# Second products of the first sub-block on whole float32 operands instead of float32r high and low parts

## The chip, the cores and the metric

The kernel runs on one core of a Trainium2 chip. The core has TensorE for matrix products (PE in the profile, its weight loads PEld), VectorE (DVE), ScalarE (ACT), GpSimd (POOL), and SyncE (SP), from whose queue the transfers start. The metric is device time in microseconds (us), from one execution of the whole program. Lower is better.

## What is computed

Chunked attention (64 tokens to a chunk, 8 heads of 64), and on its output a mixture of four experts, all in float32:

```python
scores = scale * np.matmul(q_c, k_c.transpose(0, 1, 2, 4, 3))
attn = softmax(scores)                       # with 1e-9 added to the sum
x = np.matmul(attn, v_c) ...                 # x: 4608 tokens x 512
p = domain_probs / (domain_probs.sum(-1, keepdims=True) + 1e-09)
for e in range(4):
    h = np.maximum(x @ w1[e], 0.0)           # w1[e]: 512 x 1024
    out += p[:, e:e + 1] * (h @ w2[e])       # w2[e]: 1024 x 512
```

## The kernel before

A float32 value is held as two float32r parts: the high part is what a copy into a float32r tile leaves (ACT, `hi_part`), the low part is the value less the high part (POOL or DVE, `lo_part`). A product of two such pairs is three products of parts, high by high, high by low and low by high, summed in one PSUM bank. `TERMS` at line 459 lists the three; `product` at line 463 issues one `nc.tensor.matmul` for each entry of its list, and every one of them shows up as line 465 in the profile.

The 4608 tokens are cut into 9 sub-blocks of 512. Weights are taken in 8 passes (4 experts, each in two halves of 512 hidden units; `n_pass` is 8, `n` counts passes on through the whole run). The first sub-block goes alone, in passes 0 to 7 (`startup` and `plain_pass`); the other eight go in four pairs, by a seven-product scheme on 2 by 2 blocks (`Group`, `Outer`). While PE works on the first sub-block, the attention of the first pair is computed beside it: its small steps are put between the large products by `Beside.go`, at a fixed rate. Nothing is reordered at run time; the program order on each engine is that in which the Python code issues the work.

A plain pass of the first sub-block has eight steps. Four steps are hidden blocks (`plain_hidden`, 128 hidden units by 512 tokens, twelve products each), whose result is put through ReLU by `relu_parts`: ACT writes the high part (line 472), DVE the low part (line 473). Four steps are token tiles (`Tile.whole`, 128 tokens by 512 outputs): for each of the four hidden blocks the transposed h is the stationary operand, 128 by 128, and a row block of w2 the moving one, 128 by 512. With three terms that is twelve products for a tile. Pass 0 issues tile 0 in three pieces instead, in `startup`, and the last tile of pass 7 is held back and issued as `held` within the first pass of the pairs. `Tile.out` then adds the tile, scaled by its probability, on DVE (lines 760 and 762). The pairs' own passes 8 to 15 use `Tile` as well, for 8 tiles each.

The parts of w2 are made from the loaded quarters (`raw`, tile `wraw`) by `w2_split`: four ACT copies (line 278) and four subtractions on POOL (line 281) a pass, 128 by 512 each. The tiles of h and of w2 share a family of names: `hfh0` to `hfh3` and `hfl0` to `hfl3` hold h, `hfh4`, `hfh5`, `hfl4` and `hfl5` hold w2, so that in the trace a product of a token tile reads `hfh,hfh`, `hfl,hfh` or `hfh,hfl` (names are shown without their numbers; the first is the stationary operand or the moving one, in no order that matters here). Products of hidden blocks read `xh,wf` or `xl,wf`.

Some products run on whole float32 operands already: the attention's scores (`a_scores` line 140, `start_scores` line 832) and values (`a_values` line 169, `start_values` line 852), 64 by 64 by 64 each, one call a product, and the transposes (lines 160 and 838, 128 by 128).

`product` and the two functions that set the size of the work to be followed:

```python
TERMS = ((0, 0), (0, 1), (1, 0))
...
def whole(self):
    self.part(range(NK), slice(0, dm), True, True)
```

Of the kernel before, what the change touches and what calls it, by code (L numbers as in the profile page):

```python
# [8 lines left out]
F32 = mybir.dt.float32  # L9
# [6 lines left out]
P = 128  # L16
C = 64
SUB = 512
# [12 lines left out]
def chunk_attention_moe(ctx: ExitStack, tc: tile.TileContext, qk, v, v0, dp, w1, w2, out):  # L31
# [14 lines left out]
    n_pass = 2 * n_exp  # L46
# [9 lines left out]
    hpool = ctx.enter_context(tc.tile_pool(name="hpool", bufs=1))  # L56
# [202 lines left out]
    raw = {}  # L259
    w1t, w2t = {}, {}  # L260
# [16 lines left out]
    def hi_part(src, t):  # L277
        nc.scalar.copy(out=t[0], in_=src)  # L278
# [21 lines left out]
    def w2_quad(f, k):  # L300
        return [t[:, :, f * 2 * P : (f + 1) * 2 * P] for t in w2t[k]]

    def w2_split(f, k, eng=None):
        if f == 0:
            w2t[k] = [hpool.tile([P, 2, SUB], F32R, name=f"hf{part}{4 + k}") for part in ("h", "l")]
        split(eng or nc.gpsimd, raw[1, f, k], w2_quad(f, k))

    class Factors:


# [157 lines left out]
                skip_group_check=not (first and last),  # L468
            )

    def relu_parts(src, hi, lo):
        nc.scalar.activation(out=hi, in_=src, func=AF.Relu)
        nc.vector.scalar_tensor_tensor(
            out=lo, in0=src, scalar=0.0, in1=hi.bitcast(F32), op0=ALU.max, op1=ALU.subtract
        )
# [2 lines left out]
    hs = {}  # L478
    acc = {}

    def h_alloc(s, f):
        i, k = divmod(f, 2)
        if k == 0:
            hs[s, i] = [hpool.tile([P, 2, SUB], F32R, name=f"hf{part}{2 * s + i}") for part in ("h", "l")]
        return h_part(s, f)

# [4 lines left out]
    def plain_hidden(f, tiles, alloc=True, order=BY_BLOCK, name=None):  # L491
        cols = slice(tiles[0] * P, (tiles[-1] + 1) * P)
        if alloc:
            h_alloc(0, f)
        out = bank(name)[:, : cols.stop - cols.start]
        product(
            out, order,
            lambda k, a: w1t[f // 2, k // 2][a][:, f % 2, k % 2],
            lambda k, b: xt["plain"][b][:, k, cols],
        )  # L500
        relu_parts(out, *(part[:, cols] for part in h_part(0, f)))
# [225 lines left out]
    class Tile:  # L727
# [7 lines left out]
        def part(self, fs, cols, first, last):  # L735
            if first:
                self.ps = bank(self.name)[:, : cols.stop - cols.start]
            product(
                self.ps, [(f, a, b) for f in fs for a, b in TERMS],
                lambda f, a: h_part(self.s, f)[a][:, self.i * P : (self.i + 1) * P],  # L740
                lambda f, b: w2t[f // 2][b][:, f % 2, cols],
                first=first, last=last,
            )
            if last:
                self.out(cols)
# [127 lines left out]
    def start_hidden(u, fs, lo):  # L873

        for a in range(1 if lo else 2):
            for f in fs:
                begin = u == 0 and not lo and a == 0
                if begin:
                    hidden[f] = bank(("C0", "C1", "A0", "B0")[f])[:, first]
                    h_alloc(0, f)  # L880
                product(
                    hidden[f], [(k, a, int(lo)) for k in (2 * u, 2 * u + 1)],
                    lambda k, a: w1t[f // 2, k // 2][a][:, f % 2, k % 2],
                    lambda k, b: xt["plain"][b][:, k, first],
                    first=begin, last=u == 1 and lo,
                )
# [36 lines left out]
    def startup(beside):  # L923
        load_all()
        x_alloc(0)

        nc.scalar.activation(out=small.tile([P, 1], F32, name="first"), in_=zeros[:, :1], func=AF.Exp)
        keep_warm(WAITS["loads"])
        start_scores(0)
        less_max(sc[0])  # L930
        a_exp(sc[0])
        start_scores(1)
        start_weights(0)
        less_max(sc[1])
        keep_warm(WAITS["softmax"])
        start_transpose(0)
        a_exp(sc[1])
        w1_split(0, 0, nc.gpsimd)
        keep_warm(WAITS["copy"])
        start_values(0)  # L940
        hi_part(*start_x(0))
        w1_split(1, 0, nc.gpsimd)
        start_weights(1)
        start_hidden(0, (0, 1), False)
        lo_part(nc.vector, *start_x(0))
        start_transpose(1)
        start_hidden(0, (0, 1), True)
        w1_split(0, 1, nc.gpsimd)
        start_scores(2)
        less_max(sc[2])  # L950
        start_values(1)
        hi_part(*start_x(1))
        a_exp(sc[2])
        start_hidden(0, (2, 3), False)
        start_hidden(0, (2, 3), True)
        w1_split(1, 1, nc.gpsimd)
        lo_part(nc.vector, *start_x(1))
        start_weights(2)
        w_load(1, 0, 0, 1)
        w_load(1, 0, 1, 1)  # L960
        start_v(2)
        w2_split(0, 0)
        w2_split(1, 0)
        start_hidden(1, (0, 1), False)
        start_hidden(1, (0, 1), True)
        for f in range(2):
            start_relu(f)
        w2_split(0, 1)
        w2_split(1, 1)
        start_scores(3)  # L970
        less_max(sc[3])
        start_hidden(1, (2, 3), False)
        start_transpose(2)
        start_hidden(1, (2, 3), True)
        for f in range(2, NK):
            start_relu(f)
        a_exp(sc[3])
        start_weights(3)
        norm_probs()
        o = tiles(0, 0, range(NT), ("C0", "C1", "C1", "A1"))  # L980
        o[0].part((0, 1), slice(0, dm), True, False)
        start_values(2)
        split(nc.vector, *start_x(2))
        o[0].part((2,), slice(0, dm), False, False)
        start_transpose(3)
        o[0].part((3,), slice(0, dm), False, True)
        start_values(3)
        split(nc.vector, *start_x(3))
        o[1].whole()
        beside.load()  # L990
        w_loads(0, 1)
        for f in range(NK):
            plain_hidden(f, [2, 3], alloc=False, name=("B1", "B0", "A0", "C0")[f])
        for i, (f, k) in enumerate(QUADS):
            w1_split(f, k, (nc.gpsimd, nc.vector)[i % 2])
        w_loads(1, 1)
        for i in range(2, NT):
            o[i].whole()
# [36 lines left out]
    def plain_pass(n, beside, x, ahead_of=None):  # L1035

        at = {}
        o = tiles(0, n, range(NT), ("A1", "B1", "C0", "C1") if ahead_of else None)
        steps = [lambda f=f: plain_hidden(f, range(NT)) for f in range(NK)]
        steps += [i.whole for i in o]  # L1040
        order = PAIR_QUADS if ahead_of else QUADS
        for i in range(NK):
            add(at, i // 2, lambda i=i: w2_split(*QUADS[i]))
            add(at, i // 2, lambda i=i: w_load(0, n + 1, *order[i]))
        if n == 2:
            add(at, 1, probs_by_expert)
            add(at, 5, transpose_probs)
        if not ahead_of:
            for i, (f, k) in enumerate(QUADS):
                add(at, (3, 4, 4, 5)[i], lambda f=f, k=k: w1_split(f, k, nc.gpsimd))  # L1050
            add(at, 5, lambda: w_loads(1, n + 1))
            if x:
                add(at, 0, x.sum1)
                add(at, 1, x.sum3, lambda: x.hi("t1"))
                add(at, 2, lambda: x.lo("t1"), lambda: x.hi("b22"))
                add(at, 4, lambda: x.lo("b22"))
                add(at, 5, x.sum2, lambda: x.hi("t3"))
                add(at, 6, lambda: x.lo("t3"), lambda: x.hi("t2"))
                add(at, 7, lambda: x.lo("t2"))
            issue(steps, at, beside, True)  # L1060
            return None, None
        w = []
        add(at, 0, x.sum4, lambda: x.hi("t4"))
        add(at, 1, lambda: x.lo("t4"))
        add(at, 2, lambda: w.append(Factors(0)), lambda: w[0].sum1(), lambda: w[0].sum2())
        add(at, 3, lambda: w[0].hi("a11"), lambda: w[0].hi("s2"), lambda: x.hi("b11"))
        add(at, 3, lambda: w[0].lo("a11"), lambda: w[0].lo("s2"), lambda: x.lo("b11"))
        add(at, 4, lambda: w[0].hi("a12"), lambda: x.hi("b21"), lambda: w[0].hi("s1"))
        add(at, 4, lambda: w[0].lo("a12"), lambda: x.lo("b21"), lambda: w[0].lo("s1"))
        add(at, 5, lambda: w[0].hi("a22"), lambda: w[0].lo("a22"))  # L1070
        add(at, 5, lambda: w[0].sum3(), lambda: w[0].sum4())
        add(at, 2, ahead_of.load)
        add(at, 6, lambda: w_loads(1, n + 1, order))
        issue(steps[:-1], at, beside, True)
        return steps[-1], w[0]
# [362 lines left out]
```

## Time and profile before

| | |
|---|---|
| median of two runs | 1515.2 us (1514.97 and 1515.43) |
| the profiled execution's own time | 1515.59 us |
| its span, first to last instruction | 1513.8 us |
| PE busy | 1505.7 us, 99% of the span, 8854 instructions |
| DVE, ACT, POOL busy | 918.6, 572.9 and 871.7 us |
| first sub-block | from the start to about 214 us |

The profile is that of one execution. A row of a group names the line of the kernel, the engine, the operation, the tiles as out<-in, shapes and types, the count, then the busy time, the mean duration of one in ns, and the idle time before. The durations of matmuls overlap on a pipelined PE: how long one occupies PE is read from the distance between starts, not from its duration. float32r operands of a product are printed as f32 in the PE rows, like float32 ones. In the timeline a row is a run of like instructions: start, length, engine, line and what it does.

### The profile page before, as it was taken

What the parts mean: (1) busy time and instruction counts of PE and PEld (TensorE: products, weight loads), DVE (VectorE), ACT (ScalarE), POOL (GpSimd) and SP (SyncE); (2) the same over time, 40 slices, a digit from 0 to 9 for tenths busy, and PEclk for the clock granted to TensorE, in tenths of its full rate; (3) what the DMA queues carried; (4) which work ended last, traced back from release to release, by engine and by line L of the source; (5) the groups of instructions that cost most, each with busy time, mean ns of one, the idle gap of its engine ahead of it and who ended that gap; (6) DMA issues with size and microseconds to landing.
All of it is one profiled execution on the core that took longest, in us unless ns stands there. A gap on an engine that the chain in (4) does not pass through costs nothing.

```text
span 1513.8 us, 23370 instructions
## 1 busy us (share of the span) xinstructions
PE 1505.7 (99%) x8854; PEld 1238.8 (82%) x8855; DVE 918.6 (61%) x1289; ACT 572.9 (38%) x1000; POOL 871.7 (58%) x666
## 2 busy tenths in 40 slices
PE   9999999999999999999999999999999999999998
PEld 7888888888888888888888888888888888888887
DVE  5443554444444465776766956666668756666665
ACT  3333444344444334333333444333333443333332
POOL 2443588677766616555556754555557555555554
PEclk9999999999999999999999999999999999999999
DMA  6443359877767576767665677676666676666664
GB/s 197 133 156 125 106 167 310 274 251 243 231 234 238 187 266 215 230 209 228 205 203 189 216 226 243 205 229 209 212 190 200 204 231 201 201 200 201 200 191 145
DMA packets 167936, 314.17 MB, mean 208 GB/s; under 512 B 14208, under 2 KB 84112, under 8 KB 167824
## 3 DMA queue, kind: packets, MB, share of 16 engines
q1 hardware_dynamic: 167824, 312.68, 63.7%
q8 instruction: 70, 1.15, 0.3%
q14 instruction: 42, 0.34, 0.1%
HBM read 244.39 MB, written 68.23 MB: 207 GB/s over the span
## 4 chain that ended last, share of the span: by engine, by line
PE 99%; DVE 0%; ACT 0%; issue 0%; ACTq 0%
PE A L465 49%; PE C L465 29%; PE B L465 16%; PE psa L169 1%; PE psa L140 1%; PE psa L160 1%; PE psa L780 0%; PE C L901 0%; PE B L852 0%; PE A L832 0%; PE C L780 0%; PE A L852 0%; PE psa L832 0%; PE B L838 0%; PE psa L838 0%; PE B L780 0%
## 5 line engine op out<-in xcount | busy, mean ns | idle before, releaser
L647 POOL TENSOR_TENSOR hfl<-wraw,hfh 128x512 fp32r<-128x512 f32 x288 | 374.4, 1316 | 216.2 <-ACT hfh L644 214.0
L465 PE MATMUL A<-xh,wf 128*128 128x512 f32 (+1 forms) x1104 | 379.5, 389 | 0.0
L465 PE MATMUL A<-hfh,wf 128*128 128x512 f32 (+1 forms) x768 | 270.6, 394 | 0.0
L644 ACT CAST hfh<-wraw 128x512 fp32r<-128x512 f32 x288 | 176.4, 622 | 208.5 <-DVE wraw L638 59.7
L465 PEld LDWEIGHTS A<-xh,wf 128*128 128x128 f32 x1104 | 206.8, 188 | 43.1
L527 ACT COPY s<-A 128x512 f32<-128x512 f32 x192 | 112.8, 587 | 329.7 <-PE A L465 328.9
L465 PE MATMUL A<-xl,wf 128*128 128x512 f32 (+1 forms) x552 | 213.7, 388 | 0.0
L465 PE MATMUL C<-xh,wf 128*128 128x512 f32 (+1 forms) x600 | 204.0, 388 | 0.7 <-ACT xh L278 0.7
L465 PEld LDWEIGHTS A<-hfh,wf 128*128 128x128 f32 x768 | 144.1, 188 | 31.0 <-DVE acc L694 1.2
L694 DVE TENSOR_TENSOR acc<-A,acc 128x512 f32<-128x512 f32 x174 | 119.2, 686 | 78.7 <-PE A L465 78.2
L465 PE MATMUL A<-hfl,wf 128*128 128x512 f32 x384 | 149.4, 389 | 0.0
L465 PE MATMUL C<-hfh,wf 128*128 128x512 f32 x384 | 133.9, 390 | 0.0
L281 POOL TENSOR_TENSOR hfl<-wraw,hfh 128x512 fp32r<-128x512 f32 x64 | 85.9, 1372 | 80.5 <-ACT hfh L278 80.5
L465 PEld LDWEIGHTS C<-xh,wf 128*128 128x128 f32 x600 | 111.5, 188 | 23.9 <-ACT xh L278 0.8
L465 PE MATMUL B<-xh,wf 128*128 128x512 f32 (+1 forms) x376 | 125.3, 384 | 0.0
L281 POOL TENSOR_TENSOR wf<-wraw,wf 128x512 fp32r<-128x512 f32 x70 | 91.5, 1330 | 53.4 <-ACT wf L278 53.2
L465 PEld LDWEIGHTS A<-xl,wf 128*128 128x128 f32 x552 | 103.5, 188 | 21.1
L465 PE MATMUL C<-xl,wf 128*128 128x512 f32 (+1 forms) x300 | 114.7, 385 | 0.0
L638 POOL TENSOR_TENSOR wf<-wraw,wf 128x512 f32<-128x512 f32 x23 | 29.7, 1291 | 145.2 <-DVE wf L632 145.2
L694 DVE TENSOR_TENSOR acc<-C,acc 128x512 f32<-128x512 f32 x90 | 62.2, 691 | 64.3 <-PE C L465 58.7
L647 POOL TENSOR_TENSOR hfl<-wf,hfh 128x512 fp32r<-128x512 f32 x48 | 71.2, 1483 | 38.9 <-ACT hfh L644 38.6
L465 PEld LDWEIGHTS C<-hfh,wf 128*128 128x128 f32 x384 | 72.1, 188 | 14.9
(186 smaller groups left out, 2727.7 us busy)
## 6 DMA issues: line engine op xcount, KB each, us to landing
wf<-w SPq DMA_DIRECT2D x336, 512.0 KB, 4.1
wraw<-in_w SPq DMA_DIRECT2D x128, 256.0 KB, 4.0
w<-wf SPq DMA_DIRECT2D x112, 256.0 KB, 4.7
qk_in<-in_qk SPq DMA_DIRECT2D x32, 512.0 KB, 5.4
v_in<-in_v SPq DMA_DIRECT2D x32, 256.0 KB, 4.4
w<-hfl SPq DMA_DIRECT2D x32, 256.0 KB, 2.7
w<-hfh SPq DMA_DIRECT2D x32, 256.0 KB, 2.9
w<-hfh SPq DMA_DIRECT2D x48, 128.0 KB, 2.7
```

The lines of the kernel that those rows point to most:

```text
L140: nc.tensor.matmul(s["sc"][half, c, j], lhsT=s["x"][rows, g, 0, h], rhs=s["x"][rows, g, 1, h], start=True, stop=True,)
L160: nc.tensor.transpose(ps[:, j], s["e"][:, j].rearrange("p c k -> p (c k)"), ident)
L169: nc.tensor.matmul(av[half, c, j], lhsT=s["v"][rows, 2 * j + odd], rhs=s["pt"][rows, j, half], start=True, stop=True,)
L281: eng.tensor_tensor(out=t[1], in0=src, in1=t[0].bitcast(F32), op=ALU.subtract)
L465: nc.tensor.matmul(out, lhsT=lhs(k, a), rhs=rhs(k, b), start=first and i == 0, stop=last and i == len(parts) - 1, skip_group_check=not (fi ...
L527: nc.scalar.copy(out=t, in_=self.a)
L638: (eng or nc.vector).tensor_tensor(out=self.values[place, k], in0=self.values[a, k], in1=self.values[b, k], op=op)
L644: nc.scalar.copy(out=self.part(name, 0)[:, k], in_=self.values[name, k])
L647: (eng or nc.gpsimd).tensor_tensor(out=self.part(name, 1)[:, k], in0=self.values[name, k], in1=self.part(name, 0)[:, k].bitcast(F32), op=A ...
L694: nc.vector.tensor_tensor(out=acc[key], in0=src, in1=acc[key], op=ALU.add)
```

## The change

In passes 0 to 7, h and w2 of the token tiles are kept as one float32 tile each in place of a float32r pair. `relu_parts` writes one part and returns; `w2_whole` takes the place of `w2_split` and copies the quarter on ACT, with no subtraction on POOL; `Tile.part` issues one product a hidden block on these float32 operands in place of three. The hidden blocks' own products stay as they are, and so does everything from pass 8 on.

```diff
+    def w2_whole(f, k):
+
+        if f == 0:
+            w2t[k] = [hpool.tile([P, 2, SUB], F32, name=f"hfh{4 + k}")]
+        hi_part(raw[1, f, k], w2_quad(f, k))
+
...
-    def relu_parts(src, hi, lo):
+    def relu_parts(src, hi, lo=None):
         nc.scalar.activation(out=hi, in_=src, func=AF.Relu)
+        if lo is None:
+            return
         nc.vector.scalar_tensor_tensor(
...
-    def h_alloc(s, f):
+    def h_alloc(s, f, whole=False):
         i, k = divmod(f, 2)
-        if k == 0:
+        if k == 0 and whole:
+            hs[s, i] = [hpool.tile([P, 2, SUB], F32, name=f"hfh{2 * s + i}")]
+        elif k == 0:
             hs[s, i] = [hpool.tile([P, 2, SUB], F32R, name=f"hf{part}{2 * s + i}") for part in ("h", "l")]
...
-            h_alloc(0, f)
+            h_alloc(0, f, True)
...
-                self.ps, [(f, a, b) for f in fs for a, b in TERMS],
+                self.ps, [(f, a, b) for f in fs for a, b in (TERMS if self.n >= n_pass else TERMS[:1])],
...
-        w2_split(0, 0)
-        w2_split(1, 0)
+        w2_whole(0, 0)
+        w2_whole(1, 0)
...
-            add(at, i // 2, lambda i=i: w2_split(*QUADS[i]))
+            add(at, i // 2, lambda i=i: w2_whole(*QUADS[i]))
```

The second `h_alloc(0, f, True)` is in `start_hidden`, and the other two `w2_split` calls of `startup` become `w2_whole` likewise.

More of the change, by code (lines that the diff above doesn't have):

```diff
@@ L879, in start_hidden @@
                     hidden[f] = bank(("C0", "C1", "A0", "B0")[f])[:, first]
-                    h_alloc(0, f)
+                    h_alloc(0, f, True)
                 product(
@@ L967, in startup @@
             start_relu(f)
-        w2_split(0, 1)
-        w2_split(1, 1)
+        w2_whole(0, 1)
+        w2_whole(1, 1)
         start_scores(3)
```

## The prediction

> **What bounds the kernel now.** I began with the page's first part and its chain of work, to see which engine sets the end.
>
> ```profile
> span 1513.8 us, 23370 instructions
> PE 1505.7 (99%) x8854; PEld 1238.8 (82%) x8855; DVE 918.6 (61%) x1289; ACT 572.9 (38%) x1000; POOL 871.7 (58%) x666
> PE 99%; DVE 0%; ACT 0%; issue 0%; ACTq 0%
> ```
>
> PE is busy in all but 8 us, and the chain that ended last lies on PE from end to end. The list of waits of PE says how much another engine could still give back.
>
> ```profile
> PE C L901 <- DVE s L895: 1.2, 1, 1.2
> PE A L832 <- DMA xraw<-in_qk: 0.9, 1, 0.9
> PE C L465 <- ACT xh L278: 0.7, 1, 0.7
> PE B L838 <- DVE e L198: 0.4, 1, 0.4
> PE B L1358 <- DVE acc L1352: 0.2, 1, 0.2
> PE C L901 <- issue: 0.2, 1, 0.2
> ```
>
> That is 3.6 us in all, and none of it is a wait for a low part of h or of w2. So the time of the change is the time that PE itself gains or loses on the token tiles. Last I looked at how the products of those tiles follow each other, in the chain in order of time and in the timeline around the end of the stage.
>
> ```profile
> 178.34 5.44 PE C L465 x24
> 183.78 5.44 PE A L465 x24
> ...
> 211.07 0.39 PE L465 MATMUL C<-hfh,hfh 128*128 128x512 f32 x1
> 211.07 0.19 PEld L465 LDWEIGHTS C<-hfl,hfh 128*128 128x128 f32 x1
> ```
>
> The two pieces of the chain are token tiles, two to a piece, with 24 products in 5.44 us: one float32r product of 512 columns occupies PE for 226.7 ns, and a tile of twelve for 2.72 us. The last two rows show that the weights of the next product are loaded while the present one streams.
>
> **What is removed from PE.** The instructions that touch a low part of h or w2, up to the end of the stage, in the view of the tile name hfl:
>
> ```profile
> L465 PE MATMUL C<-hfl,hfh x60: 387/389/398, 23.7 to 213.4; 128*128 128x512 f32 x60
> L465 PE MATMUL A<-hfl,hfh x48: 387/389/396, 40.9 to 202.2; 128*128 128x512 f32 x48
> L465 PE MATMUL B<-hfl,hfh x20: 389/389/389, 137.1 to 205.0; 128*128 128x512 f32 x20
> ```
>
> 60 + 48 + 20 = 128 products of one mixed kind. The code has 8 passes x 4 tiles x 4 hidden blocks = 128, and as many of each of the other two kinds, so 384 products of parts, at 226.7 ns: 87.0 us, and 32 tiles of 2.72 us. All of that is taken out and 128 float32 products of 128 x 128 by 128 x 512 are put in.
>
> **What one float32 product costs.** The trace has no float32 product of this width. It has narrow ones, and the question is how many instructions one becomes and how fast each streams. Count and duration come from the groups of PE by shape, and from the view of line 832:
>
> ```profile
> L465 PE MATMUL A<-xh,wf 128*128 128x512 f32 x1088 | 376.1, 391 | 0.0
> L465 PE MATMUL B<-xh,wf 128*128 128x256 f32 x24 | 4.6, 283 | 0.0
> L140 PE MATMUL psa<-qk_in 64*64 64x64 f32 x1024 | 20.9, 219 | 0.0
> L160 PE MATMUL psa<-ident,e 128*128 128x128 f32 x128 | 19.2, 273 | 0.0
> L832 PE MATMUL psa<-xraw x32: 218/218/267, 15.3 to 16.3; 64*64 64x64 f32 x32
> ```
>
> Count: `a_scores` calls 16 products for each of 32 tiles, 512, and the trace has 1024; one `start_scores` calls 16 and the trace has 32. A float32 product is two matmul instructions. The transposes are called 128 times and are 128, so that doubling belongs to products alone.
>
> Speed, by durations: float32r goes from 283 ns at 256 columns to 391 at 512, so 0.42 ns a column. float32 goes from 219 at 64 columns to 273 at 128, so 0.84 a column, twice that. The shapes of the two float32 rows differ, so this needs a second reading, by the time between a last product's start and the engine that waited for it:
>
> ```profile
> 183.39 0.39 PE L465 MATMUL C<-hfh,hfl 128*128 128x512 f32 x1
> 183.81 0.75 DVE L762 SCALAR_TENSOR_TENSOR acc<-C,pr,acc 128x512 f32<-128x512 f32 x1 [0.61 <-PE C L465]
> ...
> 16.33 1.10 PE L852 MATMUL B<-s,qk_in 64*64 64x64 f32 x32
> 17.48 0.59 ACT L278 CAST xh<-B 128x512 fp32r<-128x512 f32 x1 [1.39 <-PE B L852]
> ```
>
> Behind the 512-column float32r product DVE starts after 0.42 us, of which 512 x 0.42 = 215 ns is streaming and 205 the rest. The last 64-column float32 one started at 16.33 + 1.10 - 0.22 = 17.21, and ACT starts 0.27 later; 0.27 less 0.205 is 65 ns for 64 columns, about 1 ns each and nowhere near 0.42. Waits agree with durations: a float32 instruction takes two steps a column. The width of 512 then streams for 512 x 0.84 = 428 ns.
>
> Beside the streaming each instruction has a fixed part. It is 226.7 - 214 = 12.7 ns for float32r. For float32, two views of the timeline:
>
> ```profile
> 15.35 1.15 PE L832 MATMUL psa<-xraw 64*64 64x64 f32 x32
> 16.33 1.10 PE L852 MATMUL B<-s,qk_in 64*64 64x64 f32 x32
> ...
> 55.11 0.60 PE L160 MATMUL psa<-ident,e 128*128 128x128 f32 x4
> ```
>
> The 32 instructions of line 832 work on two halves of the array at once, 16 on each, and take 16.33 - 15.35 = 0.98 us: 61 ns, less 64 x 0.84 = 54 gives 7 ns. Four transposes: (0.60 - 0.27) / 3 = 109 ns, less 107 gives 2. So one wide float32 instruction occupies PE for 430 to 441 ns; I take 435, by the rows of line 832, which are products and not transposes. One product is two of them, 870 ns, against 3 x 226.7 = 680. As an outer bound, if each step over the columns paid the whole of a float32r instruction, a product would be 4 x 226.7 = 907 ns.
>
> A rule of the Trainium skill bears on this, page "FP8 and Floating Point Precision", section "TensorE Precision Notes": true float32 goes through the array in four passes, high and low of each side, all four combinations. By that rule the change is a loss on PE, four passes for three, and with whole float32r passes the sum would be +29.0 us. The trace agrees in kind, two instructions of two steps, but its rows pay the fixed part twice and not four times, so I stay with 870.
>
> **The sum.** A tile: 4 x 0.870 = 3.48 us in place of 2.72, so +0.76. Times 32 tiles: +24.3 us. With the ends of the price, 860 and 882 ns a product, it is +23.0 and +25.9, with the outer bound +29.0.
>
> **What else goes, and why it counts for nothing.** In the stage, by the view of hfl and the groups of POOL:
>
> ```profile
> L281 POOL TENSOR_TENSOR hfl<-wraw,hfh 128x512 fp32r<-128x512 f32 x32 | 45.5, 1447 | 65.3 <-ACT hfh L278 65.3
> L473 DVE SCALAR_TENSOR_TENSOR hfl<-B,hfh x15: 415/691/693, 24.5 to 197.2; 128x512 fp32r<-128x512 f32 x12, 128x256 fp32r<-128x256 f32 x3
> L473 DVE SCALAR_TENSOR_TENSOR hfl<-C,hfh x11: 415/691/693, 20.7 to 200.8; 128x512 fp32r<-128x512 f32 x8, 128x256 fp32r<-128x256 f32 x3
> L473 DVE SCALAR_TENSOR_TENSOR hfl<-A,hfh x10: 424/691/693, 24.1 to 173.7; 128x512 fp32r<-128x512 f32 x8, 128x256 fp32r<-128x256 f32 x2
> ```
>
> POOL loses 45.5 us, DVE 28 x 0.69 + 8 x 0.42 = 22.7 us. Both lie beside PE, which waited for neither: what hides them is the four hidden blocks ahead of each pass's tiles, 48 products, 10.9 us. If that cover were gone the low parts would have cost up to 68 us; it isn't, so their removal gives nothing. The quarters of w2 come free one POOL subtraction earlier, so the next loads on SP's queue can start 1.4 us sooner; PE waits for no weight load now, so that is worth nothing either. ACT's copies stay, one for one. No transfer is added, moved or taken away. No wait is added; the accumulator's DVE work behind each tile has more room than before. When PE was idle is in the view by stretches:
>
> ```profile
> 0.00:15.00 15.00, 11.67 (x128) 7.88 (x130) 7.10 (x14) 4.85 (x9) 3.25 (x8) 1.00 0.83 282
> 15.00:40.00 25.00, 24.98 (x290) 22.24 (x289) 14.37 (x30) 11.88 (x26) 8.46 (x7) 1.00 0.41 129
> ```
>
> In the first 15 us PE (the first busy time) is idle for 3.3, ahead of the first token tile, and that stays; in the next 25, which hold the first tiles, it is idle for 0.02. For these edits together I take 0, with -1 us as the better end and +1 as the worse (an alignment of the small steps beside).
>
> The profiled execution took 1515.59 us around its span of 1513.8; with 24.3 it is 1539.9. The median of the runs is 0.4 lower, so 1539.5 us, 1.6% above 1515.2.
>
> **The rivals.**
>
> *Weights in the open.* The next weights of a wide float32 product can't be loaded while it streams. What a load in the open costs is seen where the full array is taken up after small products:
>
> ```profile
> 214.53 0.50 PE L465 MATMUL A<-xh,wf 128*128 128x512 f32 x1
> 214.87 0.39 PE L465 MATMUL A<-xl,wf 128*128 128x512 f32 x1
> ```
>
> Those starts are 0.34 us apart in place of 0.227, so 0.113 us. With two loads a product and 128 products, 256 x 0.113 = 28.9 us more: 1568.4. It decides if the distance between float32 starts exceeds 0.46 us. Against it: the 7 ns beyond streaming above leave no room for a load of 64 columns, and the full array does overlap loads for float32r. The Trainium skill, page "TensorE: Matmul & The Clock Gate", part "Packing small matmuls — row/col tiling", says that a load overlaps matmuls in flight only when its row group differs; by that sentence this rival would hold, but it would hold for float32r too, and there the trace disagrees: 211.07 for the matmul and 211.07 for the next load, both on all 128 rows.
>
> *One step a column.* On the full array a wide float32 instruction streams like a float32r one. Then a product is 2 x 226.7 = 453 ns against 680, -0.227 x 128 = -29.0 us: 1486.2, on the other side. It decides below 340 ns an instruction, where the change breaks even. For it: no row shows a full-array float32 product. Against it: 219 ns and the 0.27 us release at 64 columns.
>
> *Not two but one.* The wide call is executed as one float32r pass, without the accuracy meant: 128 x (680 - 227) = 58.0 us less, 1457.2. Against it stand 1024 instructions for 512 calls.
>
> **How the numbers follow.** The forecast, two instructions of two steps, gets 0.84; weights in the open 0.08; one step a column 0.06; one pass 0.02. About 2% is what a measurement of this kernel can tell from no change: 30.3 us, or 917 ns a product. The forecast's bounds and the outer one, +29.0, all lie within 2%; I leave 0.02 of its 0.84 beyond, for a loss of the steps beside that I don't see. Slower by over 2%: 0.08 + 0.02 = 0.10. Faster by over 2%: 0.02 from the one pass and 0.02 from the one-step rival with a smaller fixed part (2 x 217 = 434 ns a product, -31.5 us), so 0.04. Within: 0.82 + 0.04 = 0.86. The range goes up to the outer bound and the worse end of the small edits, 1515.2 + 29.0 + 1 = 1545.2, given as 1546. From below the terms give 1515.2 + 23.0 - 1 = 1537.2; I widen that to 1534, because the rate of 0.84 is drawn out from 128 columns to 512, and 0.81 with no fixed part (415 ns, 830 a product, +19.2) would still fit rows rounded to a ns and a hundredth of a us. The rivals, 0.16 in all, lie outside.
>
> **What would show it.** Right: PE rows of line 465 with float32 tiles, 256 of them before about 240 us, starts 0.43 to 0.44 us apart, a pair of tiles in 6.96 us where the chain had 5.44; the first sub-block ending some 24 us later; no row of line 281 on POOL for w2 before the pairs; PE still at 99%. Wrong: starts 0.54 us apart (weights in the open) or 0.23 (one step); 128 rows in place of 256; a wait of PE on ACT's copies of w2 or on h, which would mean that the cover is gone; or a granted clock below that of before in the first 240 us.

## The result, and the profile after

The changed kernel takes 1537.03 us (two runs, 1536.84 and 1537.22) against 1515.2: a ratio of 1.0144, 95% interval 1.010 to 1.0188, +21.8 us where +24.3 was forecast. The profiled execution is the run of 1537.22 us. The page after, first part and chain:

```profile
span 1535.4 us, 23003 instructions
PE 1527.3 (99%) x8726; PEld 1215.1 (79%) x8727; DVE 892.1 (58%) x1253; ACT 572.7 (37%) x1000; POOL 825.6 (54%) x634
PE 99%; DVE 0%; ACT 0%; issue 0%; ACTq 0%
```

PE is still the chain from end to end, and it has 21.6 us more work with 128 instructions fewer (384 out, 256 in). POOL has 46 us less to do, DVE 26, and the span does not show it. The float32 products are in the view of the tile name hfh up to 240 us, and two tiles to a piece in the chain in order of time:

```profile
L471 PE MATMUL C<-hfh,hfh x120: 590/592/697, 23.4 to 235.3; 128*128 128x512 f32 x120
L471 PE MATMUL A<-hfh,hfh x96: 590/592/697, 42.4 to 222.3; 128*128 128x512 f32 x96
L471 PE MATMUL B<-hfh,hfh x40: 590/592/592, 149.1 to 225.7; 128*128 128x512 f32 x40
```

```profile
194.81 6.87 PE C L471 x16
201.68 6.87 PE A L471 x16
```

120 + 96 + 40 = 256 instructions for 128 products, so two each. 16 of them take 6.87 us: 429 ns each, 858 a product, 3.44 a tile where 2.72 stood before. The weight loads lie beside them, as these rows of the timeline after show (start, length):

```profile
195.08 0.19 PEld L471 LDWEIGHTS C<-hfh,hfh 128*128 128x128 f32 x1 [0.24 <-issue]
...
195.51 0.19 PEld L471 LDWEIGHTS C<-hfh,hfh 128*128 128x128 f32 x1 [0.24 <-issue]
```

A load of 0.19 us starts every 0.43 and PEld then idles for 0.24, while PE's stream is without a gap. The granted clock is 1.00 in every stretch up to 240 us. The stage itself is measured from the first token tile to the scores that follow the last one, before and after:

```profile
23.47 0.40 PE L465 MATMUL C<-hfh,hfh 128*128 128x512 f32 x1
...
213.91 0.69 PE L140 MATMUL psa<-qk_in 64*64 64x64 f32 x32
```

```profile
23.37 1.88 PE L471 MATMUL C<-hfh,hfh 128*128 128x512 f32 x4
...
235.84 0.69 PE L140 MATMUL psa<-qk_in 64*64 64x64 f32 x32
```

190.44 us became 212.47, so the stage is 22.0 us longer and the span 21.6: its first token tile starts 0.1 us earlier, and 0.3 us are given back behind the first sub-block.

### The profile page after: what moved, and what is told of

It is laid out like the page before. It is cut to its first block, busy times and chain, and to the rows that moved or that the text cites. A ratio compares the mean times of both kernels' runs of the same rounds, so it can differ in the third digit from the quotient of the medians.

```text
span 1535.4 us, 23003 instructions
## 1 busy us (share of the span) xinstructions
PE 1527.3 (99%) x8726; PEld 1215.1 (79%) x8727; DVE 892.1 (58%) x1253; ACT 572.7 (37%) x1000; POOL 825.6 (54%) x634
## 4 chain that ended last, share of the span: by engine, by line
PE 99%; DVE 0%; ACT 0%; issue 0%; ACTq 0%
PE A L471 49%; PE C L471 29%; PE B L471 16%; PE psa L169 1%; PE psa L140 1%; PE psa L160 1%; PE psa L790 0%; PE C L911 0%; PE B L862 0%; PE A L842 0%; PE C L790 0%; PE A L862 0%; PE psa L842 0%; PE B L848 0%; PE B L790 0%; PE psa L848 0%
## 5 line engine op out<-in xcount | busy, mean ns | idle before, releaser
L657 POOL TENSOR_TENSOR hfl<-wraw,hfh 128x512 fp32r<-128x512 f32 x288 | 374.4, 1316 | 216.1 <-ACT hfh L654 213.9
L471 PE MATMUL C<-hfh,hfh 128*128 128x512 f32 x216 | 92.1, 506 | 0.0
```

What stands on the lines that cost most here:

```text
L471: nc.tensor.matmul(out, lhsT=lhs(k, a), rhs=rhs(k, b), start=first and i == 0, stop=last and i == len(parts) - 1, skip_group_check=not (fi ...
L657: (eng or nc.gpsimd).tensor_tensor(out=self.part(name, 1)[:, k], in0=self.values[name, k], in1=self.part(name, 0)[:, k].bitcast(F32), op=A ...
```

## The experiments

My theory: the time is that of PE alone, a float32 product being two instructions of two steps a column, four passes over the columns in place of three, with a fixed part of a few ns. The rivals: that part of the change is a gain by POOL and DVE, hidden under a dearer product; that weight loads are part of the price; and that something in the stage other than the passes sets the pace.

**The lighter engines alone.** The changed kernel with three float32r products of the high parts:

```diff
-            w2t[k] = [hpool.tile([P, 2, SUB], F32, name=f"hfh{4 + k}")]
+            w2t[k] = [hpool.tile([P, 2, SUB], F32R, name=f"hfh{4 + k}")]
...
-                self.ps, [(f, a, b) for f in fs for a, b in (TERMS if self.n >= n_pass else TERMS[:1])],
+                self.ps, [(f, a, b) for f in fs for a, b in (TERMS if self.n >= n_pass else TERMS[:1] * 3)],
```

The tile of h is float32r likewise.

> The changed kernel with its lighter POOL and DVE, but PE's work as before: h and w2 as float32r high parts alone, and three float32r products of the high parts a hidden block (the low parts are left out, so the products are those of the high parts three times). If the time is PE's alone, the work taken from POOL and DVE is worth nothing: 1515.2 us, within 1. If the low parts had hindered PE (waits on them, or contention), under 1513, and the price of the float32 products is then higher than the +21.8 us of the change shows.

> The kernel of relief again, timed against the kernel before in five rounds, since its one execution had a first transfer that landed later (PE waited 0.6 us more for it). If POOL's and DVE's low parts cost PE nothing: a ratio of 1.000, within 0.001. If they had hindered it: below 0.999.

The first execution took 1516.2 us beside 1514.8, with PE waiting 1.5 us for its first transfer; eleven more have a median of 1514.84 and a ratio of 0.9997 (0.9988 to 1.0006). In the chain two tiles take what they took before:

```profile
178.17 5.44 PE C L471 x24
183.61 5.44 PE A L471 x24
```

The 45 us less of POOL and 26 us less of DVE in this run are worth nothing. The whole change is PE's.

**One pass.** The same edit with `TERMS[:1]` left as it is, so that one float32r product stands for a float32 one.

> One float32r product of the high parts a hidden block in place of one float32 product (the low parts are left out). If the float32 product is two instructions of 428.7 ns and nothing else holds the tiles: 128 x (857.4 - 226.7) = 80.7 us less than the changed kernel, 1456.3 us. If the tiles are then held by something other than PE (ReLU of the last hidden block, the accumulation of 0.75 us a tile on DVE): 1458 to 1465, with waits of PE on ACT or DVE.

It took 1471.3 us: 65.7 less than the changed kernel, not 80.7, and above the range of the second expectation as well. The first five of its waits of PE:

```profile
PE psa L160 <- DVE e L198: 2.5, 3, 1.9
PE A L471 <- ACT xh L278: 1.6, 1, 1.6
PE A L471 <- DVE xl L281: 1.4, 1, 1.4
PE A L842 <- DMA xraw<-in_qk: 1.3, 2, 0.9
PE psa L848 <- DVE pt L198: 1.2, 1, 1.2
```

and two of its stretches (busy PE, PEld, DVE, ACT, POOL, then the granted clock):

```profile
25.00:30.00 5.00, 3.28 (x40) 2.60 (x40) 3.77 (x11) 1.47 (x3) 0.00 (x0) 0.85 0.09 31
30.00:35.00 5.00, 5.00 (x34) 4.77 (x33) 1.19 (x2) 0.77 (x2) 0.00 (x0) 0.81 0.00 0
```

PE is idle for 16.6 us of its span where it was idle for 8.1, and after 1.7 us of idling at 25 to 30 us the clock is 0.81 for the next five. Here the cover is gone: PE waits on the attention's softmax (line 198) and on the splits of x (lines 278 and 281), which the program's order places beside the token tiles. In the kernel before, where a tile took 2.72 us, such waits were 0.4 and 0.7 us, both before the first tile. Between 150 and 175 us the chain also runs through two loads of weights (4.76 and 5.88 us), POOL and DVE. So the price of a pass is not the only thing that counts once PE's work shrinks. The 8.5 us more of idle time and an estimate of 3 us for the lower clock (0.85 and 0.81 in these rows, 0.97 from 150 to 200 us) make most of the 15 us missed; the rest I did not settle.

**Four float32r products.** The kernel before with low by low added:

```diff
-                self.ps, [(f, a, b) for f in fs for a, b in TERMS],
+                self.ps, [(f, a, b) for f in fs for a, b in (TERMS if self.n >= n_pass else TERMS + ((1, 1),))],
```

> The kernel before with a fourth float32r product, low by low, for each hidden block in the first sub-block's token tiles. 128 more at 226.7 ns: +29.0 us, 1544.2. If the float32 product is the same four passes with a smaller fixed part (two of 2 ns in place of four of 12.7), this is 4 x 226.7 - 857.4 = 49 ns a product above the changed kernel, some 6.3 us; if passes have one price in both, it equals the changed kernel at 1537.

> The kernel of four_terms once more, since its one execution ran at a granted clock of 0.69 all through. At the full clock: 1544.2 us if a fourth float32r product costs 226.7 ns, 1537 if four float32r passes have the price of one float32 product. If the low clock comes from the fourth product itself, it is there again and the time is near 2070.

The first execution took 2074 us with a granted clock of 1.0 for 7 us, then 0.65 up to about 1250 us and 0.75 to its end, so its time says nothing of the fourth product; the second, at 1.0, took 1543.7, beside 1515.5.

```profile
199.62 7.25 PE C L465 x32
206.87 7.25 PE A L465 x32
```

7.25 / 32 = 226.6 ns a product, four for 906, and 1543.7 - 1537.0 = 6.7 us above the changed kernel, as 49 ns x 128 = 6.3 say. A float32 product costs 48 ns less than four float32r ones. The Trainium skill, page "FP8 and Floating Point Precision", section "TensorE Precision Notes", has four passes for true float32. The trace agrees in the time, 858 ns being 4 x 214.5; what each pass multiplies no run here shows.

**Narrower pieces.** Each float32 product cut into pieces of 128 columns, then of 256. (These two kernels do not add up the full result. By the code the place is tile 0 of pass 0, the only one whose pieces are all started, in one bank, before the first of them is finished; that this is the whole of it is not shown. The instructions are all there: 1024 of 128 columns in the first run.)

```diff
+            for c in range(0, SUB, WIDE) if self.n < n_pass else (0,):
+                piece = slice(c, c + (WIDE if self.n < n_pass else SUB))
...
+                    self.ps[:, piece],
...
+                    lambda f, b: w2t[f // 2][b][:, f % 2, piece],
```

> Each float32 product of 512 columns is cut into four of 128 columns: eight instructions with a weight load each, in place of two. By a fixed part of 2 ns an instruction and loads that lie wholly beside streaming: starts 109 ns apart, 8 x 108.7 = 870 ns a product in place of 857, +1.6 us, 1538.6. By the 7 ns that I had predicted: 8 x 113.7 = 910, +6.7, 1543.7. By loads of 107 ns that don't overlap the streaming of 107: 1712 a product, +109, 1646.

> Each float32 product of 512 columns in two pieces of 256: four instructions in place of two. In the pieces of 128 columns starts were 111.7 ns apart. If that was the pace of the weight loads (107 and 5) and the streaming itself has a fixed part of only 2 ns, then at 256 columns, where loads are hidden, starts are 213.3 + 2 = 215 ns apart, 861 a product, +0.5 us on the changed kernel: 1537.5. If 5 ns is the fixed part of any float32 instruction of narrow width, starts are 218.3 apart, 873 a product, +2.0: 1539.

They took 1542.5 and 1537.55 us. Two tiles in the chain, 64 instructions of 128 columns and 32 of 256:

```profile
205.80 7.15 PE A L472 x64
```

```profile
194.97 6.91 PE C L472 x32
201.87 6.91 PE A L472 x32
```

128 columns go at 111.7 ns, 256 at 215.9, 512 at 429.4. From 256 to 512 that is 0.834 ns a column, and a line through these two has a fixed part of 2 x 215.9 - 429.4 = 2.4 ns; at 128 columns 111.7 - 106.7 = 5.0 are left. The run in pieces of 256 came out as the expectation with 2 ns said. The first of the two fits none of its three numbers; that by 7 ns is the nearest, 1.2 us off. Busy time of PE and PEld, then the granted clock, inside one piece of the chain, changed kernel and pieces of 128:

```profile
201.70:208.40 6.70, 6.70 (x17) 2.87 (x17) 1.00 0.16 49
```

```profile
205.83:212.83 7.00, 7.00 (x65) 7.00 (x64) 1.00 0.13 41
```

At 128 columns PEld has no idle time left, so it fits that the loads set the pace there, beside the stream and not in series with it. It is not shown. Width alone does not explain the 5 ns: the transposes of the kernel before, 128 columns wide too, start 109 ns apart, 2.5 above the stream, and their loads take 140 ns by their records where those of the pieces take 190. The Trainium skill says that a load overlaps matmuls in flight only when its row group differs (page "TensorE: Matmul & The Clock Gate", part "Packing small matmuls — row/col tiling"). The traces disagree: with all 128 rows in use, a product in eight pieces takes 8 x 111.7 = 894 ns, of which 8 x 106.7 = 854 are streaming, and 40 ns leave no room for eight loads in the open.

**Whose are the 13 ns?** Three float32r products cost 680 ns and not 3 x 216, and that decides how much four passes lose. So the token tiles on bfloat16 high and low parts, three products as before:

```diff
+    def halves(name):
+        t = hpool.tile([P, 2, SUB], F32, name=name).bitcast(BF16)
+        return [t[:, :, part * SUB : (part + 1) * SUB] for part in range(2)]
...
+            w2t[k] = halves(f"hfh{4 + k}")
+        hi, lo = w2_quad(f, k)
...
+                self.ps, [(f, a, b) for f in fs for a, b in TERMS],
```

> The first sub-block's token tiles on bfloat16 high and low parts, three products a hidden block as in the kernel before (the parts hold 8 bits each, so the products are coarser). float32r starts are 226.7 ns apart, 13 over the streaming of 213.3; float32 has 2 over an instruction. If the 13 ns belong to float32r: starts 215 to 216 ns apart, 384 x 11 = 4.2 us less than before, 1510.9. If they belong to any product that streams one step a column: 1515.

1510.59 us, ratio 0.9967 (0.9954 to 0.9979). Token tiles and hidden blocks of that run, one piece of each:

```profile
174.53 5.20 PE C L478 x24
...
190.37 5.44 PE C L478 x24
```

The bfloat16 tiles go at 216.7 ns by the piece (starts are 216.0 apart), the hidden blocks, still float32r, at 226.7. So the 13 ns come with float32r and not with every product of one step a column. Longer weight loads do not explain them: by their records a load takes 98 ns in bfloat16 and 188 in float32r, but in float32 it takes 190, and the pieces of 256 columns went at 215.9 with it. Why float32r pays them stays open. The Trainium skill (page "TensorE: Matmul & The Clock Gate", part "What happens when you issue a matmul", section "Back-to-back issue gap") gives N / 2.4 + 2.5 ns as the distance between single matmuls at full clock. By this an estimate for 512 columns is 215.8 ns: the trace agrees for bfloat16, and for float32 if its two steps are counted as 1024 columns (an estimate of 429.2 against 429.4), and not for float32r. For a stream of loads and matmuls the same section has about 131 ns at 512 columns; no stream here comes near it.

**A mixture.** High by high in float32r, the two products with a low part in bfloat16, in the same order:

```diff
+                self.ps, [(f, a, b) for f in fs for a, b in (TERMS if self.n >= n_pass else ((0, 0), (1, 2), (2, 1)))],
```

> The first sub-block's token tiles with high by high in float32r and the two products with a low part in bfloat16, for which a bfloat16 copy of the value is made as well (32 more copies on DVE, 36 more ReLUs on ACT, beside PE). If the 13 ns belong to float32r: 256 products at 215.5 in place of 226.7, -2.9 us against before, 1512.2. If not, 1515. Above 1516 if PE pays for the change of type between products or waits for the copies.

It took 1546.2 us (1541.3 to 1547.6), a ratio of 1.0189 (1.0174 to 1.0204; the medians alone give 1.020), the dearest of those at a clock near 1.0. From its chain, from the timeline inside the first of these pieces, and from its stretches (busy PE, PEld, DVE, ACT, POOL, then the granted clock):

```profile
160.14 5.43 PE B L479 x24
...
176.72 0.69 DVE hfl L491
...
195.50 2.96 DVE hfl L320 x2
```

```profile
162.51 0.58 PE L479 MATMUL B<-hfh,hfh 128*128 128x512 f32 x1
162.93 0.61 PE L479 MATMUL B<-hfl,hfl 128*128 128x512 bf16 x2
163.19 0.59 PE L479 MATMUL B<-hfh,hfh 128*128 128x512 f32 x1
163.61 0.61 PE L479 MATMUL B<-hfl,hfl 128*128 128x512 bf16 x2
163.87 0.58 PE L479 MATMUL B<-hfh,hfh 128*128 128x512 f32 x1
```

```profile
40.00:100.00 60.00, 54.79 (x398) 36.31 (x397) 35.47 (x49) 24.43 (x51) 22.30 (x17) 0.94 0.32 102
```

Two things went wrong. Where PE has no wait, three products still take 163.19 - 162.51 = 0.68 us, as three of float32r do: alternating the types gives back the whole of what bfloat16 saves. Even the second of two bfloat16 products in a row starts 226 ns after the first; why stays open. And DVE, with the copies and the low parts, entered the chain, where the changed kernel has PE alone. That makes the 31 us above the kernel before: PE idles for 27.8 us of its span in place of 8.1, and its busy time is 11.0 us longer, with a granted clock of 0.86 to 0.98 in the stretches from 15 to 240 us.

**All parts in bfloat16.** The bfloat16 parts of the token tiles, put to the whole program: every float32r tile becomes bfloat16, and the weights kept in DRAM with them.

```diff
-F32R = mybir.dt.float32r
...
-        t = wpool.tile([P, 2, *UNIT[1:]], F32R, name=f"wf{k}")
+        t = wpool.tile([P, 2, *UNIT[1:]], BF16, name=f"wf{k}")
```

> The kernel before with every float32r high and low part of the whole program in bfloat16, three products as before (coarser: two parts of 8 bits each; the attention stays in float32). In bf16_parts starts were 216.0 ns apart, in float32r 226.7. If that difference holds for all of some 6240 products of 512 columns: 6240 x 10.7 = 66.8 us less, 1448.5. If another engine or the weights' transfers then set the end: 1465 to 1500, with waits of PE. If the denser stream lowers the granted clock, above that, with a clock under 1.0.

1438.86 us, ratio 0.950 (0.9487 to 0.9512), the fastest version of all, and 10 us below what I expected. PE still sets its end:

```profile
span 1437.0 us, 23151 instructions
PE 1428.7 (99%) x8855; PEld 683.3 (48%) x8855; DVE 902.5 (63%) x1289; ACT 570.5 (40%) x1000; POOL 798.6 (56%) x666
```

```profile
163.51 5.18 PE B L464 x24
168.69 5.18 PE C L464 x24
```

Every large product goes at 216. DMA moved 197 MB in place of 314, but PE waited 1 us for transfers in both kernels. The 10 us are in the baseline: I had subtracted the pace of an undisturbed float32r stream, 226.7. The distances of all 6097 large products of 512 columns that are followed by another large one add up to 1394.9 us in the trace of before, 228.8 each, and to 1316.8 here, 216.0 each: 78 us. Some 65 of them are the 10.7 ns a product. Another 9 us lie at 90 places where such a stream starts behind small products: there the first distance is 323 ns in float32r and 220 in bfloat16.

**The change once more.**

> The changed kernel once more, in five rounds on the same chip as relief_2 and all_bf16. By 857.4 ns a product in place of 3 x 226.7 and some, +21.5 to +22.2 us, a ratio of 1.0142 to 1.0147.

1536.72 us beside 1515.15, a difference of 21.6; ratio 1.0148 (1.0134 to 1.0162; the medians alone give 1.0142).

## Why the prediction was right, and where a size was off

*PE is the bound and nothing else is worth anything*: right. The lighter kernel without the float32 products is at 0.9997 of before.

*Two instructions, two steps a column*: right. 256 rows for 128 products, and 429 ns where one step would have been near 227. The rate was drawn out from 64 and 128 columns, from instructions of two shapes; it held at 512 (0.834 ns a column where I had 0.84).

*The fixed part*: the term that was mis-sized. I took 7 ns from the products of line 832 over the 2 from the transposes, for being products. It is 2.4 ns at 256 and 512 columns. Some 3 of the 7 are not a fixed part at all: the pairs of line 832 start 58 ns apart, but the first distance, where the shape changes, is 107, and I had spread it over the sixteen. The other 4 to 5 are also what pieces of 128 columns pay, and the wide products do not. So 429 ns in place of 435, 858 a product in place of 870, and 12 ns x 128 = 1.5 us too much. The lower end of my price, 860, taken from the transposes, was the better value.

*The 87.0 us removed*: a little too small. The stage grew by 22.0 us while the new tiles take 32 x 3.435 = 109.9, so by this sum the old ones had taken 87.9, 229 ns a product. The chain pieces from which I read 226.7 are tiles with no small products near them; behind such products float32r starts are further apart, as in these rows of the timeline of before:

```profile
55.47 0.48 PE L465 MATMUL C<-hfh,hfh 128*128 128x512 f32 x1
55.78 0.40 PE L465 MATMUL C<-hfl,hfh 128*128 128x512 f32 x1
56.02 0.40 PE L465 MATMUL C<-hfh,hfl 128*128 128x512 f32 x1
56.25 0.40 PE L465 MATMUL C<-hfh,hfh 128*128 128x512 f32 x1
```

The distances are 0.31, 0.24 and 0.23 in place of 0.227. A first distance that is some 0.1 us longer the changed kernel has too (0.53 in place of 0.43 at half of these places). The surplus of the ones after it, 0.5 us over the token tiles of before, is gone there: its later distances have a mean of 429.1 ns. That is 0.5 of the 0.9 us. The rest I can't place; the stage is 0.3 us shorter in relief_2 than in before, with the same products. Together with 0.1 us at the start and 0.3 behind the stage, 24.3 - 1.5 - 0.9 - 0.4 = 21.5, against 21.6 in the spans; since the 0.9 was found by subtraction, this sum had to close.

*Weights in the open*: out. PEld idles for 0.24 of each 0.43 us, and starts lie 0.43 us apart and not 0.54. *One step a column* and *one pass*: out by the count and by the pace; what one pass would cost was run, and it is 1471 and not my 1457, because I had taken the tiles' time as free to shrink.

*The cover*: I named the four hidden blocks as what hides the low parts, and that taking these away gave nothing agrees with it, but I did not name the second thing that the tiles themselves cover, the softmax steps and splits beside them. The change lengthened the tiles, so it did not matter here; the one-pass run, with its waits on these steps, shows it.

## What to carry to other kernels

Where one engine is the whole chain, price a change in instructions of that engine by the distance between their starts, and take the mean over the stage for what is removed, not the cleanest stretch. A fixed part read from narrow instructions need not hold for wide ones: leave out the first distance of a row, and read it at the width in question. Float32 operands buy one call in place of three and simpler code for POOL and DVE, but 858 ns of PE in place of 680; where two parts of 8 bits are enough, bfloat16 parts at 216 ns are the cheaper way.

## What the runs showed of the hardware

A float32r product of 512 columns takes 226.7 ns from start to start where a bfloat16 one takes 216.0 and a quarter of a float32 one 214.5; with the first distances behind small products (323 ns against 220), that is most of the 78 us, 5%, by which PE's work differs between the kernel before and the one all in bfloat16. float32r and bfloat16 products in turn, in one bank, keep the pace of float32r (5.43 us for 24). One execution of one kernel on a single core had a granted clock of 0.65 and later 0.75 in all but the first 7 of its 2072 us, and the same kernel had 1.0 the next time; why stays open.
